# Attention head mixing feeding two feed-forward layers: one spread per head and chunk, and a new order of steps

## The chip, the cores and the metric

One core of a Trainium2 chip runs the whole program as one launch. The metric is the device time of one execution in microseconds (us). Engines are called PE or TensorE (matrix products), DVE or VectorE, ACT or ScalarE, POOL or GpSimd, and SP, whose queue issues most of the DMA transfers here.

## What is computed

```python
# q, k, v: (2, 12, 448, 64); w_pre, w_post: (12, 12)
scores = scale * np.matmul(q, k.transpose(0, 1, 3, 2))
scores = np.einsum('bhij,hg->bgij', scores, w_pre)
scores = scores - np.max(scores, axis=-1, keepdims=True)
attn = np.exp(scores)
attn = attn / (np.sum(attn, axis=-1, keepdims=True) + 1e-09)
attn = np.einsum('bhij,hg->bgij', attn, w_post)
attn_out = np.matmul(attn, v)             # then (896 tokens, 768)
# layer 1: h = x @ w_in (2048 wide), g = h * clip(h + 3, 0, 6) / 6, x = g @ w_out
# layer 2: h = x @ w_in, g = P(h) / (Q(h) + 1e-6) with a cubic P and a quadratic Q, out = g @ w_out
```

The 12 heads are mixed with each other before and after the softmax, for every pair of a query and a key.

## The kernel before, in words

The 448 queries of each batch are cut into chunks of 120, 120, 120 and 88 rows (the last padded to 90), eight chunks in all, called 0 to 7. A chunk is worked in groups of 10 queries: 12 groups, or 9 in chunks 3 and 7. A group has 120 rows on the partitions, 10 queries times 12 heads, so that a 120 x 120 block matrix mixes the heads in a matrix product.

Scores come out of TensorE head by head (queries on the partitions), and a group needs all heads of its queries side by side. `scores` (L233) computes a pair of heads, ScalarE and VectorE copy one head each into a staging tile `stg` (L249, L250), and `spread` (L227) sends that tile's rows by DMA to the rows of all groups. Before the change this takes two transfers for each head and chunk, one for each half of the groups:

```python
for f, (_, ng) in enumerate(spans[C]):
    to = halves[C][f].rearrange("(i h) g s -> h i g s", h=H)[h]
    nc.sync.dma_start(out=to[:, :ng], in_=st[f * HR : f * HR + ng * GR])
```

There are four `stg` buffers and three `half` tiles of six groups each. All spreads go through SP's queue, which issues in the order of the program; an issue waits until its staging tile is written.

The attention part is written out by hand as steps, one per group, in a manual schedule (from L513). Step m splits group m+2 into two float32r parts on GpSimd (`gsplit`, L255: `sh`, then `sl`), mixes group m in three products (`premix`, L270: tile `M`), takes its row maximum on VectorE (L279) and its exponential with the sum on ScalarE (L281), normalizes group m-2 on VectorE (`norm`, L286: `wr`), and mixes it again on TensorE (`postmix`, L297: tile `A`, copied to `at` by ScalarE). Into these steps tables put other work. `SST` (L510) tells at which steps of a chunk the six score pairs of the next chunk are computed (their copies and spreads follow one step later), `AVST` (L511) the six products of attention and values of the chunk before (`av_unit`, L317: tile `X`, a pair of heads each), and `QST` (L509) the split of the next chunk's queries. `k_prep` splits keys into `kst` tiles: batch 0 into XH, batch 1 into a tile of its own. Values are loaded as three tiles of four heads for a whole batch (`load_v`, L121).

The result of attention, x, must stand in XH and XL (two float32r parts) for the feed-forward layers. For chunks 0 and 1 it is first kept whole in `x1` (240 tokens, `XRAW`), since XH still holds keys, and split by `x_split` (L453, run in chunk 5); chunks 2 to 7 are split as they leave PSUM (L345, L346). In chunk 7 the first weights are loaded and split as well (`split_pieces`: two or three operations per piece on ScalarE, VectorE and GpSimd), and the first products of layer 1 begin. From there to the end the feed-forward layers run, which the change does not touch.

Of the kernel before, what the change touches and what calls it, by code (L numbers as in the profile page):

```python
# [30 lines left out]
def plan():  # L31

    chunks, halves = [], []
    for b in range(B):
        for c in range(NCH):
            n = min(CH, S - c * CH)
            G = (n + GR - 1) // GR
            chunks.append((b, c * CH, n, G))  # L40
# [6 lines left out]
def fused_kernel(  # L47
# [177 lines left out]
    halves = {}  # L225

    def spread(C, h, st):  # L227

        for f, (_, ng) in enumerate(spans[C]):
            to = halves[C][f].rearrange("(i h) g s -> h i g s", h=H)[h]  # L230
            nc.sync.dma_start(out=to[:, :ng], in_=st[f * HR : f * HR + ng * GR])  # L231

    def scores(C, hp, tags=("sc", "sc")):  # L233
# [613 lines left out]
```

## Time and profile before

| | us |
|---|---|
| median of 3 runs | 798.34 (797.26 to 799.27) |
| profiled execution | 793.91 |
| its span | 792.1 |
| first mixing product of group 0 starts | 33.85 |
| attention part ends (last values multiplied) | about 307 |
| TensorE busy in the span | 724.5 (91%) |
| VectorE, ScalarE, GpSimd busy | 567.2, 402.4, 258.0 |

Busy time of TensorE is modelled and an average over parts with different limits. The attention part is read step by step: a view of the waits or of the chain tells which engine's or queue's work ended last before a product could start.

### The profile page before, as it was taken

What the parts mean: (1) busy time and instruction counts of PE and PEld (TensorE: products, weight loads), DVE (VectorE), ACT (ScalarE), POOL (GpSimd) and SP (SyncE); (2) the same over time, 40 slices, a digit from 0 to 9 for tenths busy, and PEclk for the clock granted to TensorE, in tenths of its full rate; (3) what the DMA queues carried; (4) which work ended last, traced back from release to release, by engine and by line L of the source; (5) the groups of instructions that cost most, each with busy time, mean ns of one, the idle gap of its engine ahead of it and who ended that gap; (6) DMA issues with size and microseconds to landing.
All of it is one profiled execution on the core that took longest, in us unless ns stands there. A gap on an engine that the chain in (4) does not pass through costs nothing.

```text
span 792.1 us, 12221 instructions
## 1 busy us (share of the span) xinstructions
PE 724.5 (91%) x4457; PEld 621.5 (78%) x4457; DVE 567.2 (72%) x1036; ACT 402.4 (51%) x765; POOL 258.0 (33%) x255
## 2 busy tenths in 40 slices
PE   4397998889789889999999999999999998999986
PEld 2276776567577678888888888888999887999975
DVE  3366555366765576986674555568999999999996
ACT  3264555455555544444432111126676666689872
POOL 1275575465637581644442444420000000000000
PEclk9598999999999999999999999999999999999999
DMA  6631422324441512533332333323534343411002
GB/s 215 174 102 52 122 57 72 89 80 118 110 121 30 150 56 71 162 116 117 120 102 79 110 113 111 107 96 120 156 92 153 119 152 108 156 64 61 1 1 80
DMA packets 58747, 81.51 MB, mean 103 GB/s; under 512 B 5340, under 2 KB 54048, under 8 KB 58688
## 3 DMA queue, kind: packets, MB, share of 16 engines
q1 hardware_dynamic: 56768, 79.15, 32.7%
q10 hardware_dynamic: 1856, 1.58, 0.7%
q8 instruction: 35, 0.57, 0.3%
q14 instruction: 24, 0.20, 0.1%
q0 software_dynamic: 64, 0.01, 0.1%
HBM read 58.62 MB, written 2.75 MB: 77 GB/s over the span
## 4 chain that ended last, share of the span: by engine, by line
PE 58%; DVE 21%; DMA 10%; SPq 4%; issue 3%; ACT 3%; POOL 2%; POOLq 0%; ACTq 0%; DVEq 0%
PE h L355 8%; PE h L357 8%; PE h L356 8%; DMA half<-stg 6%; PE A L308 6%; PE y L355 5%; PE y L356 5%; PE y L357 5%; SPq L231 4%; PE X L328 3%; PE sc L246 3%; PE M L275 2%; DMA wraw<-in_moe_w_in_dram 2%; PE M L277 2%; DVE u L684 2%
## 5 line engine op out<-in xcount | busy, mean ns | idle before, releaser
L355 PE MATMUL h<-xh,wh 128*128 128x512 f32 (+1 forms) x384 | 141.6, 369 | 2.1 <-ACT wh L417 1.1
L357 PE MATMUL h<-xh,wl 128*128 128x512 f32 (+1 forms) x384 | 140.8, 368 | 2.1 <-DVE wl L418 2.1
L356 PE MATMUL h<-xl,wh 128*128 128x512 f32 (+1 forms) x384 | 140.7, 366 | 0.0
L281 ACT ACTIVATE e<-M,st 120x448 f32<-120x448 f32 x90 | 57.2, 635 | 105.5 <-DVE st L279 87.1
L308 PEld LDWEIGHTS A<-wr,e 120*112 120x112 f32 x720 | 87.6, 182 | 29.1 <-ACT at L312 8.0
L279 DVE TENSOR_REDUCE st<-M 120x1 f32<-120x448 f32 x90 | 56.0, 623 | 74.5 <-PE M L277 74.1
L308 PE MATMUL A<-wr,e 120*112 120x120 f32 x720 | 93.7, 275 | 14.8 <-DVE wr L292 12.8
L399 ACT ACTIVATE wf<-wraw 128x768 f32<-128x768 f32 (+1 forms) x50 | 43.7, 875 | 123.9 <-POOL wl L415 103.2
L265 POOL TENSOR_TENSOR sl<-half,sh 120x448 fp32r<-120x448 f32 x89 | 103.4, 1161 | 7.4
L263 POOL TENSOR_SCALAR sh<-half 120x448 fp32r<-120x448 f32 x89 | 54.8, 615 | 122.1 <-DMA half<-stg 69.9
L357 PEld LDWEIGHTS h<-xh,wl 128*128 128x128 f32 x384 | 72.1, 188 | 11.8 <-DVE wl L418 3.3
L355 PEld LDWEIGHTS h<-xh,wh 128*128 128x128 f32 x384 | 72.1, 188 | 11.5 <-ACT wh L417 1.9
L401 DVE TENSOR_SCALAR wf<-wf 128x768 int32<-128x768 int32 (+1 forms) x50 | 27.3, 546 | 74.4 <-ACT wf L399 74.1
L356 PEld LDWEIGHTS h<-xl,wh 128*128 128x128 f32 x384 | 72.1, 188 | 8.2
L414 POOL TENSOR_SCALAR wh<-wf 128x768 fp32r<-128x768 f32 (+1 forms) x34 | 33.4, 983 | 129.7 <-PE y L356 55.9
L355 PE MATMUL y<-gh,wh 128*128 128x384 f32 x192 | 70.6, 368 | 0.0
L356 PE MATMUL y<-gl,wh 128*128 128x384 f32 x192 | 70.2, 366 | 0.0
L357 PE MATMUL y<-gh,wl 128*128 128x384 f32 x192 | 69.7, 363 | 0.0
L415 POOL TENSOR_TENSOR wl<-wf,wh 128x768 fp32r<-128x768 f32 (+1 forms) x34 | 65.6, 1931 | 2.8
L275 PE MATMUL M<-sh,wp_h 120*120 120x448 f32 x90 | 43.0, 478 | 22.1 <-DVE sh L263 11.9
L312 ACT ACTIVATE at<-A 112x480 f32<-112x480 f32 x90 | 51.8, 576 | 4.4 <-PE A L308 4.0
L407 DVE SCALAR_TENSOR_TENSOR wf<-wraw,icst,wf 128x768 int32<-128x768 int32 (+1 forms) x50 | 50.5, 1012 | 0.8
(115 smaller groups left out, 1527.2 us busy)
## 6 DMA issues: line engine op xcount, KB each, us to landing
wraw<-in_moe_w_in_dram SPq DMA_DIRECT2D x30, 768.0 KB
wraw<-in_moe_w_out_dram SPq DMA_DIRECT2D x28, 768.0 KB
half<-stg SPq DMA_DIRECT2D x168, 105.0 KB
wraw<-in_moe_w_out_dram SPq DMA_DIRECT2D x6, 512.0 KB
kraw<-in_k_dram SPq DMA_DIRECT2D x6, 448.0 KB
vraw<-in_v_dram SPq DMA_DIRECT2D x6, 448.0 KB
qraw<-in_q_dram SPq DMA_DIRECT2D x6, 360.0 KB
wraw<-in_moe_w_in_dram ACTq DMA_DIRECT2D x2, 768.0 KB
```

Source lines behind the costliest of these rows:

```text
L263: eng.tensor_scalar(out=sh[:r], in0=s[:r], scalar1=1.0, scalar2=0.0, op0=ALU.mult, op1=ALU.add)
L265: return eng.tensor_tensor(out=sl[:r], in0=s[:r], in1=sh[:r].bitcast(F32), op=ALU.subtract)
L275: nc.tensor.matmul(mt[:r, :S], lhsT=a[:r, :r], rhs=sh[:r], start=True, stop=False)
L279: nc.vector.tensor_reduce(out=st[:r, 0:1], in_=mt[:r, :S], op=ALU.max, axis=AX.X, negate=True)
L281: nc.scalar.activation(out=e[:r], in_=mt[:r, :S], func=AF.Exp, bias=st[:r, 0:1], accum_out=st[:r, 1:2])
L308: nc.tensor.matmul(av[:, jc], lhsT=e[:r, jc * JP : (jc + 1) * JP], rhs=wr[:r, :, :rr], start=True, stop=True)
L312: lambda: nc.scalar.activation(out=at[C][:, :, :, c0 : c0 + rr], in_=av, func=AF.Copy)
L355: nc.tensor.matmul(o, lhsT=wh, rhs=mh, start=first, stop=False)
L356: nc.tensor.matmul(o, lhsT=wh, rhs=ml, start=False, stop=False)
L357: nc.tensor.matmul(o, lhsT=wl, rhs=mh, start=False, stop=last)
L407: nc.vector.scalar_tensor_tensor(out=wi, in0=lw, scalar=icst[:, 1:2], in1=wi, op0=ALU.logical_shift_right, op1=ALU.bitwise_or)
L415: nc.gpsimd.tensor_tensor(out=lv, in0=w, in1=hv.bitcast(F32), op=ALU.subtract)
```

## The change

Names: `full` is the tile that takes the place of the two `half` tiles, `stage` one tile for all heads of chunk 0.

- A chunk's groups stand in one tile `full` (two buffers), and a head's rows of a whole chunk go there in one transfer. Only chunk 0 still has two parts of six groups; its first part is sent first for all heads, eight heads by SP and four by ScalarE's queue.
- Scores of chunk 0 are staged at once in `stage`, which lies in one of the two `at` buffers. Later chunks stage a pair of heads in one tile of the tag `raw`, five buffers that the key loads share.
- Keys of batch 1 are split into XL, and loaded and split two pairs of heads at a time at steps 8 to 11 of chunks 0 to 2. So x stays whole in `x1` for chunks 0 to 5 (688 tokens). ScalarE makes the high part of the first 568 in chunk 6; the rest and the low part of all 688 follow in chunk 7.
- Values are loaded by pairs of heads for every chunk, each load behind the product that frees its buffer.
- The tables: score pairs at steps 0, 1, 3, 4, 6, 7 (of 9: 0 to 5), the queries of the chunk after next split at steps 8 and 9 (of 9: 6 and 7), value products at 2, 5, 8, 9, 11, 11. In a step VectorE's part of the copies now stands ahead of `premix`.

```diff
-            halves.append([(0, HG), (n - rest * GR, rest)])
+            parts.append([(0, G)] if chunks else [(0, HG), (HG, G - HG)])
...
-    XRAW = 2 * CH
+    XRAW = S + 2 * CH
...
-        t = front.tile([128, 2, S], F32, tag="raw", bufs=3, name=f"kraw{b}_{m}")
+        t = front.tile([128, 2, S], F32, tag="raw", bufs=5, name=f"kraw{b}_{m}")
...
-    def load_v(b, m):
-        t = att.tile([JP, 4, JC * D], F32, tag="vraw", bufs=3, name=f"vraw{b}_{m}")
+    def load_v(C, hp):
+        if C < len(chunks):
+            t = att.tile([JP, 2, JC * D], F32, tag="vraw", bufs=3, name=f"vraw{C}_{hp}")
+            nc.sync.dma_start(out=t, in_=v[chunks[C][0], hp])
...
-        front.tile([128, 2, NP, S], F32R, name="kst1"),
+    ksts = [x.rearrange("p c t -> p (c t)").rearrange("p (x h s) -> p x h s", x=2, s=S) for x in (XH, XL)]
...
+    def spread(C, h, st, part=0, eng=nc.sync):
+        g0, ng = parts[C][part]
+        to = full[C].rearrange("(i h) g s -> h i g s", h=H)[h]
+        eng.dma_start(out=to[:, g0 : g0 + ng], in_=st[g0 * GR : (g0 + ng) * GR])
...
-            halves[C] = [
-                att.tile([GP, HG, S], F32, tag="half", bufs=3, name=f"half{C}_{f}") for f in range(len(spans[C]))
-            ]
+            full[C] = att.tile([GP, MG, S], F32, tag="full", bufs=2, name=f"full{C}")
...
-        st = [front.tile([CH, S], F32, tag="stg", bufs=4, name=f"stg{C}_{2 * hp + i}") for i in range(2)]
+        if far:
+            st = front.tile([CH, 2, S], F32, tag="raw", bufs=5, name=f"stg{C}_{hp}")
...
+        load_v(*((C, h // 2 + 3) if h // 2 + 3 < NP else (C + 1, h // 2 + 3 - NP)))
         if h % 4 == 3:
             av_evac(C, h, X)
...
+    stage = att.tile([CH, H, S], F32, tag="at", bufs=2, name="stage")
     k_prep(0, 0)
     flush()
-    q_prep(0)
+    q_prep(0, 0, 1)
...
+        scores(0, hp, (("M", "A"), ("sc", "sc"))[hp % 2], stage[:, 2 * hp : 2 * hp + 2])
         flush()
+        if hp < 4:
+            for h in (2 * hp, 2 * hp + 1):
+                spread(0, h, stage[:, h])
+    for h in range(8, H):
+        spread(0, h, stage[:, h], 0, nc.scalar)
+    for h in range(H):
+        spread(0, h, stage[:, h], 1)
...
+    def x_hi(c, a, b):
+        nc.scalar.activation(out=XH[:, c, a:b], in_=x1[:, c, a:b], func=AF.Copy)
...
-            lambda: nc.scalar.activation(out=o, in_=x1[:, c, :], func=AF.Copy),
+            lambda: x_hi(c, XEAR, XRAW),
             lambda: nc.vector.tensor_tensor(
-                out=XL[:, c, :XRAW], in0=x1[:, c, :], in1=o.bitcast(F32), op=ALU.subtract
+                out=XL[:, c, :XRAW], in0=x1[:, c, :], in1=XH[:, c, :XRAW].bitcast(F32), op=ALU.subtract
...
-    QST = {12: 1, 9: 0}
-    SST = {12: [3, 4, 5, 6, 7, 8], 9: [3, 3, 4, 4, 5, 5]}
-    AVST = {12: [2, 2, 5, 9, 10, 11], 9: [2, 3, 5, 6, 8, 8]}
+    SST = {12: [0, 1, 3, 4, 6, 7], 9: [0, 1, 2, 3, 4, 5]}
+    QST = {12: [8, 9], 9: [6, 7]}
+    AVST = {12: [2, 5, 8, 9, 11, 11], 9: [2, 3, 5, 6, 8, 8]}
...
             gsplit(m + 2)
-            premix(m)
             for p in todo:
                 p[1]()
+            premix(m)
...
-            if C == NCH + 1 and s < KD:
+            if nxt is None and s < KD:
                 x_split(s)
+            if nxt == len(chunks) - 1 and s < KD:
+                x_hi(s, 0, XEAR)
```

The order of the instructions, at three places. **ScalarE at the start** (`sc` is a score tile, `qraw` and `kraw` are loaded queries and keys). Before:

```order
L249 ACTIVATE stg_0_142<-sc_0_140 120x448
L212 ACTIVATE xh<-kraw_2_107 128x448
L249 ACTIVATE stg_2_160<-sc_2_158 120x448
L212 ACTIVATE xh<-kraw_2_107 128x448
L249 ACTIVATE stg_4_178<-sc_4_176 120x448
L249 ACTIVATE stg_6_196<-sc_6_194 120x448
L221 ACTIVATE qr<-qraw_109 128x720
```

With the change:

```order
L212 ACTIVATE xh<-kraw_1_105 128x448
L249 COPY stage<-sc_0_131 120x448
L212 ACTIVATE xh<-kraw_1_105 128x448
L249 COPY stage<-sc_2_147 120x448
L212 ACTIVATE xh<-kraw_2_107 128x448 x2
L249 COPY stage<-sc_4_161 120x448
L249 COPY stage<-sc_6_175 120x448
L249 COPY stage<-sc_8_189 120x448
L231 DMA full_130<-stage 10x6x448
L249 COPY stage<-sc_10_201 120x448
L231 DMA full_130<-stage 10x6x448 x3
L221 ACTIVATE qr<-qraw_109 128x720
```

Four of chunk 0's first spreads now stand in ScalarE's own stream, behind its last copies; the other 20 stand in SP's.

**SP's queue in a later chunk** (the scores of chunk 2, computed during chunk 1). Before:

```order
L113 DMA qraw_746<-in_q_dram 128x6x90
L231 DMA half_0_734<-stg_0_738 10x6x448
L231 DMA half_1_735<-stg_0_738 10x6x448
L231 DMA half_0_734<-stg_1_739 10x6x448
L231 DMA half_1_735<-stg_1_739 10x6x448
```

With the change:

```order
L117 DMA qraw_585<-in_q_dram 128x6x90
L231 DMA full_611<-stg_0_614 10x12x448 x2
L231 DMA full_611<-stg_1_649 10x12x448 x2
L128 DMA vraw_3_692<-in_v_dram 112x512
L231 DMA full_611<-stg_2_718 10x12x448 x2
L231 DMA full_611<-stg_3_753 10x12x448 x2
L128 DMA vraw_4_794<-in_v_dram 112x512
```

A pair of heads takes two issues instead of four, and loads of values stand between them.

**VectorE in the last chunk**, around its steps 3 and 4. Before:

```order
L292 TENSOR_SCALAR wr_3202<-wq,st_3156 120x120
L279 TENSOR_REDUCE st_3212<-M_3208 120x1
L401 TENSOR_SCALAR wf<-wf 128x768
L403 SCALAR_TENSOR_TENSOR wf<-wraw,icst,wf 128x768
L289 TENSOR_SCALAR st_3178<-st_3178 120x1
L290 RECIPROCAL st_3178<-st_3178 120x1
L292 TENSOR_SCALAR wr_3235<-wq,st_3178 120x120
L279 TENSOR_REDUCE st_3245<-M_3241 120x1
```

With the change:

```order
L294 TENSOR_SCALAR wr_3125<-wq,st_3074 120x120
L478 TENSOR_TENSOR xl<-x_86,xh 128x688
L281 TENSOR_REDUCE st_3136<-M_3132 120x1
L406 TENSOR_SCALAR wf<-wf 128x768
L408 SCALAR_TENSOR_TENSOR wf<-wraw,icst,wf 128x768
L291 TENSOR_SCALAR st_3098<-st_3098 120x1
L292 RECIPROCAL st_3098<-st_3098 120x1
L294 TENSOR_SCALAR wr_3162<-wq,st_3098 120x120
L351 TENSOR_TENSOR xl<-X_1_3110,xh 128x2x120
L478 TENSOR_TENSOR xl<-x_86,xh 128x688
L281 TENSOR_REDUCE st_3174<-M_3170 120x1
```

A subtraction over 688 columns stands ahead of the reduce in six steps of this chunk.

## Rows read from the trace of the kernel before

**Rows 1.** The page: the engines' busy time (share of the span), and the clock that TensorE was granted in 40 equal slices (tenths of full speed).

```profile
PE 724.5 (91%) x4457; PEld 621.5 (78%) x4457; DVE 567.2 (72%) x1036; ACT 402.4 (51%) x765; POOL 258.0 (33%) x255
...
PEclk9598999999999999999999999999999999999999
```

**Rows 2.** The chain of waits around the change from chunk 1 to chunk 2: start, duration, what.

```profile
91.57 0.05 issue
91.62 0.75 SPq L231
...
97.41 2.55 DMA half<-stg
...
102.06 0.48 PE M L277
```

**Rows 3.** The tile view of `half`: the issues (duration in ns, least, median, most), and who waited for the tile and the spreads (us, times).

```profile
L231 SPq DMA_DIRECT2D half<-stg x192: 748/749/970, 11.5 to 269.5; - x192
...
  POOL sh L263: 69.9, 7
...
  DVE stg L250: 25.7, 18
  ACT stg L249: 23.9, 14
```

**Rows 4.** The DMA view: issues by kind, with the size of one.

```profile
half<-stg SPq DMA_DIRECT2D x168, 105.0 KB
...
half<-stg SPq DMA_DIRECT2D x24, 52.5 KB
```

**Rows 5.** SP's own timeline: start, time from the first to the last of a run of issues, line, what, how many.

```profile
43.77 20.25 SPq L231 DMA_DIRECT2D half<-stg  x24
```

**Rows 6.** Windows: stretch, its length, busy us of each engine (instructions), granted clock, busy share of the 16 DMA engines, GB/s. In this stretch SP issues spreads back to back.

```profile
28.00:32.00 4.00, 0.00 (x0) 0.00 (x0) 0.37 (x1) 0.00 (x0) 0.00 (x0) 0.50 0.45 134
```

**Rows 7.** The timeline of ScalarE at the start, then two rows of VectorE's: the split and the first reduce of group 0.

```profile
9.28 1.05 ACT L212 ACTIVATE xh<-kraw 128x448 fp32r<-128x448 f32 x2 [1.20 <-DMA kraw<-in_k_dram]
10.23 0.53 ACT L249 ACTIVATE stg<-sc 120x448 f32<-120x448 f32 x1
...
11.55 0.57 ACT L212 ACTIVATE xh<-kraw 128x448 fp32r<-128x448 f32 x1
17.65 0.54 ACT L249 ACTIVATE stg<-sc 120x448 f32<-120x448 f32 x1 [5.53 <-DMA half<-stg]
...
33.40 0.39 DVE L263 TENSOR_SCALAR sh<-half 120x448 fp32r<-120x448 f32 x1 [5.03 <-DMA half<-stg]
...
35.51 0.62 DVE L279 TENSOR_REDUCE st<-M 120x1 f32<-120x448 f32 x1 [0.82 <-PE M L277]
```

**Rows 8.** The pace of steps. TensorE's timeline: a step with a score pair (86.33 to 88.74), and one with a value pair (products `M` from 97.60, then `A`, then `X`). GpSimd's: the wait at the chunk change. VectorE's reduces: the first two of chunk 2, the first of chunk 6 and its tenth, and the first of chunk 7.

```profile
86.33 0.47 PE L275 MATMUL M<-sh,wp_h 120*120 120x448 f32 x1
...
88.74 0.46 PE L275 MATMUL M<-sh,wp_h 120*120 120x448 f32 x1
...
97.60 0.46 PE L275 MATMUL M<-sh,wp_h 120*120 120x448 f32 x1
...
99.22 1.04 PE L328 MATMUL X<-at,vraw 112*64 112x120 f32 x16
...
100.22 0.57 POOL L263 TENSOR_SCALAR sh<-half 120x448 fp32r<-120x448 f32 x1 [6.42 <-DMA half<-stg]
...
102.57 0.62 DVE L279 TENSOR_REDUCE st<-M 120x1 f32<-120x448 f32 x1 [2.87 <-PE M L277]
...
104.32 0.63 DVE L279 TENSOR_REDUCE st<-M 120x1 f32<-120x448 f32 x1
...
239.91 0.62 DVE L279 TENSOR_REDUCE st<-M 120x1 f32<-120x448 f32 x1 [3.90 <-PE M L277]
...
263.65 0.62 DVE L279 TENSOR_REDUCE st<-M 120x1 f32<-120x448 f32 x1 [0.58 <-PE M L277]
...
273.83 0.62 DVE L279 TENSOR_REDUCE st<-M 120x1 f32<-120x448 f32 x1 [3.25 <-PE M L277]
```

**Rows 9.** Windows of chunk 6 and of chunk 7 (columns as in rows 6: TensorE, weight loads, VectorE, ScalarE, GpSimd), then two lines of the source views (duration in ns, least, median, most) of subtractions on VectorE, and a row of VectorE's timeline in step 3 of chunk 7.

```profile
240.00:260.00 20.00, 19.40 (x161) 15.85 (x161) 13.60 (x37) 11.68 (x28) 13.92 (x17) 0.94 0.15 42
...
273.00:284.00 11.00, 9.20 (x79) 7.44 (x80) 7.83 (x20) 5.84 (x14) 10.25 (x13) 1.00 0.33 111
284.00:296.00 12.00, 10.14 (x87) 8.67 (x87) 9.21 (x22) 5.89 (x14) 9.09 (x9) 1.00 0.25 73
...
L457 DVE TENSOR_TENSOR xl<-x,xh x6: 886/1006/1372, 206.1 to 221.6; 128x240 fp32r<-128x240 f32 x6
...
L222 DVE TENSOR_TENSOR ql<-qraw,qr x8: 907/1116/1873, 8.1 to 245.1; 128x720 fp32r<-128x720 f32 x6, 128x540 fp32r<-128x540 f32 x2
...
281.32 1.78 DVE L403 SCALAR_TENSOR_TENSOR wf<-wraw,icst,wf 128x768 int32<-128x768 int32 x1
```

**Rows 10.** The issue of value loads (ns), two rows of the chain of waits (the six value products of the last chunk, and a load of weights), and a window of the feed-forward part.

```profile
L123 SPq DMA_DIRECT2D vraw<-in_v_dram x6: 352/418/1121, 32.5 to 200.6; - x6
...
303.65 3.79 PE X L328 x96
...
629.66 4.63 DMA wraw<-in_moe_w_in_dram
...
500.00:540.00 40.00, 40.00 (x200) 35.88 (x199) 22.75 (x31) 9.43 (x13) 10.00 (x7) 1.00 0.36 112
```

More of the change, by code (lines that the diff above doesn't have):

```diff
@@ L26 @@
 HG = 6
-HR = HG * GR
+MG = CH // GR
 NP = H // 2
 def plan():
-    chunks, halves = [], []
+    chunks, parts = [], []
     for b in range(B):
@@ L39, in plan, with row_of @@
             G = (n + GR - 1) // GR
+            parts.append([(0, G)] if chunks else [(0, HG), (HG, G - HG)])
             chunks.append((b, c * CH, n, G))
-            rest = G - HG
-            halves.append([(0, HG), (n - rest * GR, rest)])
-    return chunks, halves
+    return chunks, parts
+def row_of(chunk, g):
+    return min(g * GR, chunk[2] - GR)
 @with_exitstack
@@ L69, in fused_kernel @@
     GLAG = 1
-    chunks, spans = plan()
+    chunks, parts = plan()
     groups = [(C, g) for C, c in enumerate(chunks) for g in range(c[3])]
@@ L223, in q_prep, with scores @@
         )
[L225 to L233, printed above, removed]
+    full = {}
+    def spread(C, h, st, part=0, eng=nc.sync):
+        g0, ng = parts[C][part]
+        to = full[C].rearrange("(i h) g s -> h i g s", h=H)[h]
+        eng.dma_start(out=to[:, g0 : g0 + ng], in_=st[g0 * GR : (g0 + ng) * GR])
+    def scores(C, hp, tags=("sc", "sc"), st=None):
         n = chunks[C][3] * GR
@@ L246, in scores, with take @@
                 nc.tensor.matmul(sc[i][:n, :S], lhsT=w[o, hp, :n], rhs=x[o], start=(j == 0), stop=(j == 2))
-        post(
-            2,
-            lambda: (nc.scalar.activation(out=st[0][:n], in_=sc[0][:n, :S], func=AF.Copy), spread(C, 2 * hp, st[0])),
-            lambda: (nc.vector.tensor_copy(out=st[1][:n], in_=sc[1][:n, :S]), spread(C, 2 * hp + 1, st[1])),
-        )
+        def take(i, copy):
+            copy(out=st[:n, i], in_=sc[i][:n, :S])
+            if far:
+                spread(C, 2 * hp + i, st[:, i])
+        post(2, lambda: take(0, nc.scalar.copy), lambda: take(1, nc.vector.tensor_copy))
     ssp = {}
@@ L299, in postmix @@
         r, rr = GP, GR
-        c0 = spans[C][g // HG][0] + g % HG * GR
+        c0 = row_of(chunks[C], g)
         if g == 0:
@@ L341, in av_evac @@
         if t0 < XRAW:
-            xposts.append([lambda: None, lambda: nc.vector.tensor_copy(out=x1[:, cs, ts_], in_=src)])
+            take = [lambda: None, lambda: None]
+            take[h != 7] = lambda: (nc.vector.tensor_copy if h != 7 else nc.scalar.copy)(out=x1[:, cs, ts_], in_=src)
+            xposts.append(take)
         else:
@@ L524, in fused_kernel @@
         if nxt is not None:
-            if C > 0:
-                add([lambda: q_prep(nxt)], [QST[G]])
             add([lambda h=h: scores(nxt, h) for h in range(NP)], SST[G])
-        if C == 0:
-            add([lambda h=h: k_prep(1, h) for h in range(NP)], [0, 1, 2, 9, 10, 11])
+        if C + 2 < len(chunks):
+            add([lambda: q_prep(C + 2, 0, NP // 2), lambda: q_prep(C + 2, NP // 2, NP)], QST[G])
+        if C < 3:
+            add([lambda: load_k(1, C), lambda: k_prep(1, 2 * C), lambda: k_prep(1, 2 * C + 1)], [8, 10, 11])
         if C > 0:
@@ L539, in fused_kernel @@
         for s in range(G):
-            if s == 4 and C + 2 < len(chunks):
+            if s == 0 and C + 2 < len(chunks):
                 load_q(C + 2)
@@ L567, in fused_kernel @@
                 u()
-            if C == NCH and s == max(AVST[G]):
-                for i in range(3):
-                    load_v(1, i)
             if nxt is None and s == 0:
@@ L804, in _laid_out @@
     import numpy as _np
[L806 removed]
+    chunks, parts = plan()
     qt = _np.zeros((len(chunks), 2, D, NP, CH), q.dtype)
[L809 to L812 removed]
+    for C, (c, ps) in enumerate(zip(chunks, parts)):
+        for g0, ng in ps:
+            rows = [[c[1] + row_of(c, g0 + g) + i for g in range(ng)] for i in range(GR)]
+            rows = q[c[0], :, _np.array(rows).ravel()].reshape(ng * GR, NP, 2, D)
+            qt[C, ..., g0 * GR : (g0 + ng) * GR] = rows.transpose(2, 3, 1, 0)
     kt = k.reshape(B, NP, 2, S, D).transpose(0, 2, 4, 1, 3)
[L816 removed]
+    vt = v.reshape(B, NP, 2, JC, JP, D).transpose(0, 1, 4, 2, 3, 5)
     return {
```

35 lines of the change are left out of this document (13 added, 22 removed).

## The prediction

> **What bounds the kernel now.** I read the page first: TensorE is busy 91% of the span, and the clock line says where it isn't: the granted clock is 0.5 (the 1.2 GHz level) in the second slice, dips in the fourth, and is full later [rows 1]. So look at the attention part, from 0 to about 303 us. The chain of waits there, around one chunk change, reads: a reduce, then issue after issue on SP's queue, 0.75 us each, then a transfer of score rows, then GpSimd's split, and only then TensorE [rows 2]. The tile view of `half` sums it: 192 spreads; GpSimd waited 69.9 us for them in 7 places, the two engines that copy scores out 25.7 and 23.9 us for staging tiles still being sent [rows 3]. An issue takes 748 ns at least and 749 in the middle of all 192, though 168 move 60 rows of one head and 24 move 30 [rows 3, 4]: it costs by the piece, not by rows. SP's own timeline shows the queue saturated: 24 issues in 20.25 us from 43.77 [rows 5], against chunks of 34 us in which scores come only at steps 3 to 8. While it issues back to back the DMA engines are 0.45 busy [rows 6]. **SP's issues bound the attention part, not TensorE.**
>
> **The change, part by part.** The sum is made against the profiled execution, 793.91 us (span 792.10); the runs' median is 798.34, 0.6% above. I carry the saving over to the median.
>
> *First chunk.* Now group 0's split starts at 33.40, after 24 spreads through four staging buffers; ScalarE's third copy waited 5.53 us for one [rows 7]. After: 12 spreads carry groups 0 to 5, 8 issued by SP and 4 by ScalarE, and `stage` never blocks a copy. ScalarE is last: its first copy stays at about 10.2 (it follows the key load that lands at 9.28), then six copies at 0.53, three key splits at 0.57 and four issues at the 0.75 of SP's: 10.2 + 3.2 + 1.7 + 3.0 = 18.1, plus 2.6 from issue to landing [rows 2, 7]: 20.7, or **-12.7**. SP's eight end by 11.5 + 8 x 0.8 = 17.9 [rows 3]. Groups 6 to 11 follow on SP until about 28 and land by 31; group 6's split is due at step 4, 8 us after the first: covered. Bounds: if ScalarE's four cost as if on SP, 11.5 + 12 x 0.8 + 2.6 = 23.7 (-9.7); if ScalarE issues in half the time, -14.2.
>
> The DMA rule that the two queues end on the same 16 engines, so that a second issuer saves only sequencer time (the Trainium skill, DMA: Bandwidth & Descriptors, "Issuing engines are not separate DMA queues"), calls that time usually small; by it the ScalarE issues would bring nothing and this term would be -9.7. The trace disagrees: issuing is what fills the time, with the engines 0.45 busy [rows 6].
>
> *One spread per head and chunk.* 12 issues for 24. A 120-row issue isn't in the trace; the nearest rows (60 and 30 at the same price) give 0.75 [rows 3, 4]; the upper bound is twice that. The transfer's engine time doubles: 0.45 busy over 0.8 us becomes at most 0.8 x 0.9 = 0.72 us on 16 engines [rows 6]. So 12 take 9.6 us of SP per chunk, at the upper bound 18.6, where 24 took 20. SP also gets 6 value loads (0.42 each, [rows 10]) for each chunk, queued in the order of the attention-value products they wait for; behind them stand only spreads of later steps. 12 x 0.8 + 6 x 0.45 (with the gap between) + 0.9 for a query and a key load = 13 us in 30: SP is no longer full.
>
> On engine use, the Trainium skill (same page, "Why a DMA increments its semaphore by 16 and not by 1") lets a transfer use only as many engines as divide both outer sizes, here 10 for 120 rows onto 10 partitions. By it a spread takes 1.15 us and twelve 13.8, still under a chunk; the sum is unchanged, the upper bound comes nearer.
>
> *Step order.* Two whole `full` tiles let spreads begin at step 0, three steps (7 us) earlier, and the last pair is copied out at step 8: landed about 6.2 us into that step (copy 1.3, two issues 1.6, landing 2.6 + 0.7). GpSimd's split of the next group 0 is due 6 us into it and needed 5.2 us later: **the 6.4 us wait on GpSimd at a chunk change and its 2.9 us on VectorE go** [rows 2, 8]. The q split leaves the chunk's start for steps 8 and 9; the score copy stands before the reduce on VectorE, which waits for TensorE there anyway: nothing.
>
> What is late next is TensorE itself. Its undisturbed steps: with a score pair 86.33 to 88.74 = 2.41; with one value pair 1.62 + 1.0 = 2.6; with one of each 2.41 + 1.0 = 3.4, and with two value pairs taken as the same; with none 1.75, taken as 1.8 [rows 8]. A 12-step chunk after: 6 x 2.41 + 4 x 2.6 + 1.8 + 3.4 = 30.1; chunk 0 (no value products) 25.3; the 9-step chunk 3 x 2.41 + 3 x 3.4 + 2.6 + 1.8 + 3.4 = 25.2. Seven chunks: 25.3 + 5 x 30.1 + 25.2 = 201, against 273.83 - 35.51 = 238.3 now [rows 7, 8]. Such sums are a little short: nine steps from 239.91 took 23.7 where they give 22.4 [rows 8]. The first of them still refills after a stall, so I take half, 0.7 per nine steps: 6.3, in which chunk 0's first steps at the 1.2 GHz level (as now [rows 6]) must fit too. **-31**. Bounds: -37 without it; -20 if a third of the stalls stay.
>
> *Keys in XL, x kept raw.* Chunks 2 to 5 lose a subtraction each on VectorE and most of ScalarE's copies; chunk 6 gets six copies of 568 columns on ScalarE (some 0.7 each, as 448 take 0.57 [rows 7]; it is 11.7 of 20 us busy there [rows 9], so nothing). The last chunk gets six subtractions of 688 columns. The row of 240 columns took 0.89 to 1.37 with GpSimd running, the one of 720 0.91 to 1.87 [rows 9]: I take 1.4 each, 8.4 us. VectorE is busy 17.0 of 23 us there [rows 9], and its steps 3, 4 and 6 carry weight splits too, one of 1.78: they go above 4 us. **+5** of the 8.4, bounds 0 and +8.4.
>
> *The last values.* Three buffers hold one pair each, so pairs 3 to 5 of the last chunk load only when 0 to 2 are used. Six units take 3.79 us now [rows 10]. A load of 224 KB lands between the spread's 2.6 (105 KB) and the weights' 4.63 (768 KB) [rows 2, 10]: 2.9 by size. Unit 3 starts 0.63 + 0.1 + 0.42 + 2.9 = 4.0 in, not 1.9; less overlap of the later ones: **+1.7**, bounds 0 and +3. Behind it TensorE is full until 540 us [rows 10], so what the attention part gains or loses arrives at the end whole.
>
> Sum: -12.7 - 31 + 5 + 1.7 = **-37**: 757 by the profile, **761** on the median. Ends: -14.2 - 37 + 0 + 0 gives 747; -9.7 - 20 + 8.4 + 3 gives 780.
>
> **The rivals.**
> *A, issue grows with rows* (1.5 us). For it: a spread of 120 rows has twice the descriptors. Against: 30 and 60 rows cost the same. SP needs 18.6 + 3.6 of 30 us; the earlier start covers most, the 9-step chunk does not. About 1 us at six changes and 4 more in chunk 3: 771.
> *B, the floor is higher than TensorE's steps*: the small waits of copies, norms and splits behind each other cost 0.2 us in each of 81 steps. For it: the nine steps that ran over their sum by 1.3 us [rows 8]. 761 + 10 (0.2 x 81, less the 6.3 allowed): 771, with the last chunk's full 8.4: 775.
> *C, the split of group 0 still waits for all 24 first spreads.* Then it starts at 11.5 + 20 x 0.8 + 2.6 = 30.1, -3.3 in place of -12.7: 770. Against: it reads rows that only the first 12 write.
> *D, slower: the one big spread.* If issue and transfer of 120 rows follow each other without overlap, at 1.5 + 1.4 = 2.9 us, twelve take 35; with copy, landing and split (6) a chunk lasts 41 in place of 34: +7 x 6.8 - 6 = +42, 840. Against: issues now stand 0.05 us apart while transfers run under them [rows 2]. It decides from 2.4 us a spread: 12 x 2.4 + 6 = 34.8, where the rest's 6 us are used up.
> *E, ScalarE's issues save nothing*: its four and SP's next ones hold each other up. The first split comes at 23.7: 764. Against: the engines have room [rows 6].
> That the change doesn't do what it says is C.
>
> **How the numbers follow.** A measurement of this kernel tells 0.3% (2.4 us) from no change. Forecast 0.58 (752 to 768); A 0.10, B 0.12, C 0.06, D 0.04, E 0.08, anything near no change 0.02. Range 748 to 777: the forecast's own, E, and A, B and C with most of their width; it leaves out D and the far ends. Faster 0.94, same 0.02, slower 0.04.
>
> **What would show it.** Right: first reduce near 22.8 (35.5 now); issues of the 120-row spread at 0.75 to 0.8; GpSimd's waits for `full` under 10 us in sum; reduces of neighbouring chunks about 30 us apart and 25 in the 9-step one; no clock below 0.9 after 40 us; the last chunk 5 us longer, with VectorE as the releaser; a gap of 1 to 2 us between the last value units. Wrong: a spread issue well above 0.8, a first split near 30, steps with scores at 2.6 or more without a DMA wait.

## The result, and the profile after

The changed kernel takes 774.3 us (median of 4 runs, 771.24 to 776.24), the kernel before 797.8 beside it (4 runs, 797.09 to 799.27): ratio 0.970, 95% interval 0.9664 to 0.9735. It is faster, and the time lies in the range, but 23.5 us were saved where the forecast said 37. The profiled execution after took 776.24 (span 774.5), the longest of its four; the one of before (793.91) is shorter than all its four. So the two profiles differ by 17.6 only.

Where the time went, stage by stage. The marks are VectorE's row maxima (the first of each chunk) and the first 512-column product of layer 1; the last column runs to the span's end.

| us | to the first maximum | chunks 0 to 2 | chunks 3 to 6 | chunk 7, first to last maximum | to the first 512-column product | to the end |
|---|---|---|---|---|---|---|
| before | 35.5 | 99.8 | 138.5 | 22.2 | 13.0 | 483.0 |
| after | 23.4 | 98.8 | 118.9 | 29.7 | 17.6 | 486.1 |

The start saves 12.1 and chunks 3 to 6 save 19.6. Chunks 0 to 2 save 1.0 only, and 7.5, 4.6 and 3.1 are lost behind them.

The page after, as [rows 1]: TensorE is busy 94% now, and the clock dips in new places: most in the 14th slice (252 to 271 us), where chunk 7 runs, and again in the 34th, in layer 2.

```profile
PE 725.1 (94%) x4457; PEld 630.3 (81%) x4457; DVE 599.2 (77%) x1037; ACT 401.7 (52%) x772; POOL 256.1 (33%) x255
...
PEclk8799999999999799999999999999999998999998
```

What went as forecast: the tile view of `full` after (as [rows 3]; issues in ns, then waits in us and times), and SP's timeline (as [rows 5]), and VectorE's split and first maximum (as [rows 7]):

```profile
L231 SPq DMA_DIRECT2D full<-stg x84: 755/756/1267, 30.2 to 231.2; - x84
L231 SPq DMA_DIRECT2D full<-stage x20: 748/748/967, 9.7 to 27.8; - x20
L231 ACTq DMA_DIRECT2D full<-stage x4: 778/780/1550, 13.3 to 16.6; - x4
...
  DMA full<-stg: 5.7, 3
```

```profile
9.67 18.88 SPq L231 DMA_DIRECT2D full<-stage  x20
...
30.16 14.09 SPq L231 DMA_DIRECT2D full<-stg  x12
```

```profile
21.24 0.39 DVE L265 TENSOR_SCALAR sh<-full 120x448 fp32r<-120x448 f32 x1 [2.01 <-DMA full<-stage]
...
23.35 0.62 DVE L281 TENSOR_REDUCE st<-M 120x1 f32<-120x448 f32 x1 [0.82 <-PE M L279]
```

An issue of 120 rows takes 756 ns, as one of 60 or 30 did. GpSimd's 69.9 us for spreads [rows 3] held 30.1 at the start and 39.9 later; now it is 17.9 at the start and 5.7 later. Another 6.6 us, all ahead of a chunk's first group, are put down to loads of values and queries.

Then what did not. The end of chunk 0 after, steps 9 to 11: VectorE, ScalarE and TensorE (start, duration, what, in brackets the wait ahead of it).

```profile
48.75 0.53 DVE L222 TENSOR_TENSOR ql<-qraw,qr 128x360 fp32r<-128x360 f32 x1 [1.14 <-ACT qr L221]
49.20 0.62 DVE L281 TENSOR_REDUCE st<-M 120x1 f32<-120x448 f32 x1
...
51.59 1.56 DVE L213 TENSOR_TENSOR xl<-kraw,xl 128x448 fp32r<-128x448 f32 x1 [0.60 <-ACT xl L212]
53.08 0.61 DVE L281 TENSOR_REDUCE st<-M 120x1 f32<-120x448 f32 x1
```

```profile
49.91 0.64 ACT L283 ACTIVATE e<-M,st 120x448 f32<-120x448 f32 x1 [1.20 <-DVE st L291]
50.44 0.19 ACT L283 ACTIVATION_READ_ACCUMULATOR e<-M,st 120x1 f32 x1
50.53 0.57 ACT L314 ACTIVATE at<-A 112x480 f32<-112x480 f32 x1
50.99 0.57 ACT L212 ACTIVATE xl<-kraw 128x448 fp32r<-128x448 f32 x1
53.78 0.63 ACT L283 ACTIVATE e<-M,st 120x448 f32<-120x448 f32 x1 [2.23 <-DVE st L291]
```

```profile
51.14 1.04 PE L310 MATMUL A<-wr,e 120*112 120x120 f32 x8 [1.73 <-ACT at L314]
...
52.43 0.37 PE L279 MATMUL M<-sl,wp_h 120*120 120x448 f32 x1
55.02 1.05 PE L310 MATMUL A<-wr,e 120*112 120x120 f32 x8 [2.22 <-ACT at L314]
```

Read them as a ring. ScalarE's exponential (49.91) waits for VectorE; behind it on ScalarE stand the copy to `at` and the key split's high part (50.99). VectorE's low part (51.59) waits for that, and the next row maximum (53.08) stands behind the low part, although its product ended at 52.80. ScalarE's next exponential waits for the maximum (2.23), and TensorE for ScalarE (2.22). A step takes 3.9 us. VectorE's waits, first two lines of before, then after: the splits wait for ScalarE in more places, and the wait for the mixing product has shrunk, since the maximum comes late instead.

```profile
DVE st L279 <- PE M L277: 74.1, 60, 4.2
...
DVE ql L222 <- ACT qr L221: 4.3, 3, 3.4
```

```profile
DVE st L281 <- PE M L279: 14.4, 30, 0.9
DVE ql L222 <- ACT qr L221: 12.8, 15, 2.7
...
DVE xl L213 <- ACT xl L212: 5.2, 6, 1.6
DVE xl L478 <- ACT xh L473: 4.8, 4, 1.7
```

Chunk 7 after: a window (columns as in [rows 6, 9]), and step 3 on VectorE, with the subtraction of 688 columns ahead of the maximum, two weight pieces behind it, and then TensorE's wait.

```profile
241.00:271.00 30.00, 23.31 (x166) 19.16 (x165) 23.70 (x47) 12.92 (x34) 17.63 (x18) 0.83 0.40 115
```

```profile
250.44 0.87 DVE L478 TENSOR_TENSOR xl<-x,xh 128x688 fp32r<-128x688 f32 x1 [1.72 <-ACT xh L473]
251.23 0.62 DVE L281 TENSOR_REDUCE st<-M 120x1 f32<-120x448 f32 x1
251.76 0.79 DVE L406 TENSOR_SCALAR wf<-wf 128x768 int32<-128x768 int32 x1
252.59 1.76 DVE L408 SCALAR_TENSOR_TENSOR wf<-wraw,icst,wf 128x768 int32<-128x768 int32 x1
```

```profile
255.07 1.91 PE L310 MATMUL A<-wr,e 120*112 120x120 f32 x8 [3.39 <-DVE wr L294]
...
281.90 1.51 PE L330 MATMUL X<-at,vraw 112*64 112x88 f32 x32 [1.53 <-DMA vraw<-in_v_dram]
284.46 1.30 PE L330 MATMUL X<-at,vraw 112*64 112x88 f32 x16 [1.06 <-DMA vraw<-in_v_dram]
```

The eight products at 255.07 take 1.91 us, where eight took 1.05 at 55.02: ahead of them TensorE stood for 3.39 us, the granted clock is at its 1.2 GHz level, and the chunk's mean is 0.83. The last two rows are the forecast's gaps in the values.

### The profile page after: what moved, and what is told of

It reads as the page before. It is cut to its first block, busy times and chain, and to the rows that moved or that the text cites. A ratio compares the mean times of both kernels' runs of the same rounds, so it can differ in the third digit from the quotient of the medians.

```text
span 774.5 us, 12237 instructions
## 1 busy us (share of the span) xinstructions
PE 725.1 (94%) x4457; PEld 630.3 (81%) x4457; DVE 599.2 (77%) x1037; ACT 401.7 (52%) x772; POOL 256.1 (33%) x255
## 4 chain that ended last, share of the span: by engine, by line
PE 66%; DVE 21%; ACT 6%; DMA 4%; issue 2%; SPq 0%; DVEq 0%; ACTq 0%
PE h L360 8%; PE h L362 8%; PE h L361 8%; PE A L310 7%; PE y L360 5%; PE sc L246 5%; PE y L361 5%; PE y L362 5%; PE X L330 4%; PE M L277 3%; DVE st L281 2%; PE M L279 2%; ACT e L283 2%; PE M L278 2%; DVE u L706 2%
## 5 line engine op out<-in xcount | busy, mean ns | idle before, releaser
L360 PE MATMUL h<-xh,wh 128*128 128x512 f32 (+1 forms) x384 | 143.5, 374 | 2.1 <-DVE u L704 1.0
L362 PE MATMUL h<-xh,wl 128*128 128x512 f32 (+1 forms) x384 | 142.4, 372 | 2.1 <-DVE wl L423 2.1
L310 PEld LDWEIGHTS A<-wr,e 120*112 120x112 f32 x720 | 88.6, 182 | 33.4 <-ACT at L314 14.2
L310 PE MATMUL A<-wr,e 120*112 120x120 f32 x720 | 92.9, 274 | 22.1 <-DVE wr L294 14.3
L267 POOL TENSOR_TENSOR sl<-full,sh 120x448 fp32r<-120x448 f32 x89 | 103.8, 1166 | 7.4
L265 POOL TENSOR_SCALAR sh<-full 120x448 fp32r<-120x448 f32 x89 | 52.6, 591 | 95.9 <-PE M L278 64.3
L281 DVE TENSOR_REDUCE st<-M 120x1 f32<-120x448 f32 x90 | 55.9, 621 | 18.5 <-PE M L279 14.4
L294 DVE TENSOR_SCALAR wr<-wq,st 120x120 f32<-120x120 f32 x90 | 64.5, 717 | 3.2
## 6 DMA issues: line engine op xcount, KB each, us to landing
wraw<-in_moe_w_in_dram SPq DMA_DIRECT2D x30, 768.0 KB
wraw<-in_moe_w_out_dram SPq DMA_DIRECT2D x28, 768.0 KB
```

The costliest lines, as they stand in the source:

```text
L265: eng.tensor_scalar(out=sh[:r], in0=s[:r], scalar1=1.0, scalar2=0.0, op0=ALU.mult, op1=ALU.add)
L267: return eng.tensor_tensor(out=sl[:r], in0=s[:r], in1=sh[:r].bitcast(F32), op=ALU.subtract)
L281: nc.vector.tensor_reduce(out=st[:r, 0:1], in_=mt[:r, :S], op=ALU.max, axis=AX.X, negate=True)
L294: nc.vector.tensor_scalar(out=wr[:r], in0=wq[:r], scalar1=st[:r, 3:4], scalar2=None, op0=ALU.mult)
L310: nc.tensor.matmul(av[:, jc], lhsT=e[:r, jc * JP : (jc + 1) * JP], rhs=wr[:r, :, :rr], start=True, stop=True)
L360: nc.tensor.matmul(o, lhsT=wh, rhs=mh, start=first, stop=False)
```

## The experiments

Theory 1 is the ring. Theory 2: VectorE's `wr` (L294), 365 ns on average before and 717 after, stretches the steps. Theory 3: spreads land late. All ratios are to the kernel before, run beside each on the same chip; e1 to e3 and c0 shared one chip, e4 to e7 another, e8 to e10 a third, and e11 ran on a fourth. Stages are from one profile of each.

| kernel | median us (range) | ratio, 95% interval | chunks 0 to 2 | 3 to 6 | chunk 7 | to 512 columns |
|---|---|---|---|---|---|---|
| c0, as changed | 773.6 (769.9 to 775.8) | 0.9704, 0.966 to 0.975 | 97.2 | 118.9 | 29.7 | 16.4 |
| e1 | 765.4 (764.2 to 767.3) | 0.9608, 0.957 to 0.964 | 91.3 | 116.9 | 28.4 | 16.8 |
| e2 | 767.5 (764.8 to 769.6) | 0.9638, 0.959 to 0.969 | 91.6 | 116.9 | 28.3 | 18.0 |
| e3 = e2 + 4 value buffers | 762.4 (762.2 to 766.2) | 0.9579, 0.954 to 0.962 | 92.0 | 117.7 | 28.4 | 14.2 |
| e4 = e3 + early x split | 763.0 (762.6 to 763.3) | 0.9597, 0.958 to 0.961 | 90.7 | 119.6 | 27.6 | 14.7 |
| e5 = e3, all first spreads on SP | 762.5 (761.2 to 765.8) | 0.9596, 0.957 to 0.962 | 95.4 | 117.1 | 28.8 | 14.4 |
| e6 = e3, two spreads per head | 773.4 (770.3 to 774.5) | 0.9719, 0.969 to 0.975 | 97.4 | 117.9 | 29.7 | 14.2 |
| e7 = e3, old tables | 770.4 (768.0 to 771.0) | 0.9683, 0.966 to 0.970 | 96.7 | 120.0 | 28.5 | 14.5 |
| e8 = e3 without low part of x | 756.7 (755.0 to 757.3) | 0.9501, 0.945 to 0.955 | 90.9 | 116.9 | 22.9 | 14.4 |
| e9 = e3, x split apart | 762.7 (760.4 to 764.2) | 0.9577, 0.953 to 0.963 | 89.6 | 117.0 | 27.3 | 15.1 |
| e10 = e9 + 5 value buffers | 760.1 (758.7 to 763.1) | 0.9560, 0.950 to 0.962 | 90.4 | 117.2 | 27.5 | 14.2 |
| e11 = e10 + early x split | 762.0 (758.7 to 763.3) | 0.9588, 0.955 to 0.963 | 90.1 | 119.0 | 24.1 | 14.2 |

**c0, e1, e2: the ring.**

> The changed kernel once more, as the measure for the three beside it. All theories: 771 to 776 us, ratio to before 0.967 to 0.973.

```diff
# e1
-            for p in todo:
-                p[1]()
             premix(m)
+            for p in todo:
+                p[1]()
```

> Only the order inside a step is put back: all of VectorE's copies and subtractions stand behind the mixing product's row maximum again, as before the change; tables, spreads and buffers stay as changed. Theory 1 (a serial ring: a subtraction of the query, key or x split, which needs ScalarE's high part of the same step, holds up the row maximum, and ScalarE's next exponential behind it): chunks 0 to 2 take 87 to 90 us from first reduce to first reduce of chunk 3 in place of 98.9, the last chunk 3 to 5 us less; in all 10 to 14 us less than the changed kernel, 760 to 764, a little of it lost again because score copies leave later. Theory 2 (VectorE's normalization beside GpSimd's split, 717 ns in place of 365, is what stretches the steps): the row of the normalization stays near 700 ns and so do the chunks; within 3 us of the changed kernel, 771 to 776. Theory 3 (spreads land late in chunks 0 to 2): later copies make it worse, 775 to 785.

```diff
# e2: the subtractions carry a mark, p[2]
+            late = [p for p in todo if p[2:]]
             for p in todo:
-                p[1]()
+                if not p[2:]:
+                    p[1]()
             premix(m)
+            for p in late:
+                p[1]()
```

> Copies out of PSUM (scores, x of chunks 0 to 5) stay ahead of the row maximum as changed, but the subtractions of the query, key and x splits go behind it. Theory 1: as with everything behind it or up to 3 us better, since score copies and with them the spreads leave as early as in the changed kernel: 758 to 763; waits of the query and key subtractions on ScalarE no longer show a row maximum behind them, TensorE's gaps of 1.5 to 2.2 us in steps 8 to 11 of chunks 0 to 2 gone. Theory 2: within 3 us of the changed kernel. Theory 3: within 2 us of the changed kernel.

e1 takes 8.2 us off c0, e2 6.1, and chunks 0 to 2 fall by 5.9 and 5.6 (7.5 and 7.2 against the first profile of the changed kernel). That is theory 1, smaller than expected: chunks 0 to 2 were to take 87 to 90 us, and both totals lie 1.4 to 4.5 us above what was written down for them. The same place in e2 on VectorE; then from its waits, and `wr` from the groups (busy us, mean ns | idle before):

```profile
47.13 0.62 DVE L287 TENSOR_REDUCE st<-M 120x1 f32<-120x448 f32 x1
47.66 0.52 DVE L227 TENSOR_TENSOR ql<-qraw,qr 128x360 fp32r<-128x360 f32 x1
...
49.05 0.62 DVE L287 TENSOR_REDUCE st<-M 120x1 f32<-120x448 f32 x1 [0.29 <-PE M L285]
```

```profile
DVE ql L227 <- ACT qr L226: 3.5, 4, 2.8
```

```profile
L300 DVE TENSOR_SCALAR wr<-wq,st 120x120 f32<-120x120 f32 x90 | 60.5, 672 | 3.1
```

The step from 47.13 to 49.05 takes 1.9 us where the changed kernel needed 3.9 for the next one (49.20 to 53.08), and the query split's wait falls from 12.8 to 3.5. `wr` is about as slow as in the changed kernel (672 ns for 717; 424 in e1), and the gain is there in both: theory 2 falls. Theory 3 falls too, since e1 sends the spreads later and lost nothing. Whether copies stand ahead of the maximum (e2) or behind it (e1) makes no difference that the intervals show.

**e3: the last values.**

```diff
-            t = att.tile([JP, 2, JC * D], F32, tag="vraw", bufs=3, name=f"vraw{C}_{hp}")
+            t = att.tile([JP, 2, JC * D], F32, tag="vraw", bufs=4, name=f"vraw{C}_{hp}")
# each load four pairs ahead, four at the start
```

> The same with four value buffers in place of three, and loads four pairs ahead. If the two gaps of 1.5 and 1.1 us in the last values are the loads that wait for a free buffer, one of them goes or both shrink below 0.5: 1.5 to 3 us less than with three buffers, and if the fall of the clock behind them (0.52 for two products after) goes as well, up to 1 us more. If the loads are late for another reason (SP's queue), within 0.7 us.

The medians differ by 5.1 us. In the profiles the stretch behind the last maximum falls from 18.0 to 14.2: TensorE's wait for values shrinks from 1.68 to 0.93 us, and the granted clock over the stretch is 0.83 in e2 and 1.00 in e3, so most of the 3.8 is the clock of that one execution. e1, also with three buffers, has a wait of 1.62, a clock of 0.90 and a stretch of 16.8. The rest of the 5.1 has no place in these profiles: e3's is the longest of its four runs, and its span, 764.4, is no shorter than e2's 763.8.

**e6, e7: issue count or earlier start.**

```diff
# e6
-            parts.append([(0, G)] if chunks else [(0, HG), (HG, G - HG)])
+            parts.append([(0, HG), (HG, G - HG)])
...
-                spread(C, 2 * hp + i, st[:, i])
+                for part in (0, 1):
+                    spread(C, 2 * hp + i, st[:, i], part)
# e7
-    SST = {12: [0, 1, 3, 4, 6, 7], 9: [0, 1, 2, 3, 4, 5]}
-    QST = {12: [8, 9], 9: [6, 7]}
-    AVST = {12: [2, 5, 8, 9, 11, 11], 9: [2, 3, 5, 6, 8, 8]}
+    SST = {12: [3, 4, 5, 6, 7, 8], 9: [3, 3, 4, 4, 5, 5]}
+    QST = {12: [9, 10], 9: [6, 7]}
+    AVST = {12: [2, 2, 5, 9, 10, 11], 9: [2, 3, 5, 6, 8, 8]}
```

> The same as with four value buffers, but every head and chunk is sent in two transfers again (six groups and the rest), 24 a chunk, into the one tile and with the new tables. Theory issue count: the 24 issues take 18 us of SP again and bring back the stalls, chunks 33 to 34 us, 14 to 20 us more: 776 to 782. Theory earlier start: SP needs 24 x 0.8 + 3.5 = 22.7 of 30 us and starts three steps earlier, so chunks stay within 0.5 us of 30.5, total within 3 us, 762 to 765; only the 9-step chunk (22.7 of 26) may lose 2.

> The same as with four value buffers (one spread per head and chunk), but score pairs stand at steps 3 to 8 and value products at 2, 2, 5, 9, 10, 11 as before the change (the query split at steps 9 and 10). Theory issue count: twelve issues follow the copies without a queue, the last pair lands 6 to 6.5 us into step 9, 1 to 2 us late for the next chunk's first group: chunks 31 to 32, 5 to 9 us more, 767 to 771. Theory earlier start: stalls of 4 to 6 us at each change, on GpSimd for the spread tile, chunks 34 to 36, 24 to 35 us more: 786 to 797.

Two spreads cost 11.0 us, more than the theory of the earlier start allowed and less than that of the issue count; the old tables cost 8.0, as the issue count had it. In the profiles seven chunks take 215.3 and 216.7 us, against 209.7 in e3 and 238.3 before. So taking back either half loses only 5.6 or 7.0 of the 28.6 us that e3 gained there, and neither theory fits both runs. That fewer issues make a late start harmless, and that an early start hides many issues, would fit both, but it isn't shown: e6 and e7 both keep the two whole tiles and the five staging buffers, and no run takes back issues and tables together. In both the wait is back at the change from chunk 0 to 1, where e3's TensorE has one of 0.56 us; TensorE in e6 and e7:

```profile
52.48 0.46 PE L284 MATMUL M<-sh,wp_h 120*120 120x448 f32 x1 [3.54 <-POOL sh L272]
```

```profile
51.82 0.46 PE L283 MATMUL M<-sh,wp_h 120*120 120x448 f32 x1 [3.59 <-POOL sh L271]
```

The profile of e6 is the shortest of its four runs; its other 3 us have no place in it.

**e5: ScalarE's four issues.**

```diff
-        spread(0, h, stage[:, h], 0, nc.scalar)
+        spread(0, h, stage[:, h], 0)
```

> The same as with four value buffers, but the last four heads of chunk 0's first part are sent by SP's queue as all others, not by ScalarE's. If a second queue saves issue time (the forecast): first split at 23 to 24 in place of 21.3, so 1.7 to 3 us more: 764 to 765.5. If the transfers themselves are the limit (rival E of the prediction): first split within 0.7 us, total 762.4.

The medians are equal. From SP's first issue to the first split it is 12.2 us here (9.86 to 22.1) and 11.6 in e3 (10.57 to 22.2): ScalarE's issues save 0.6, not 3. In e3, and in the changed kernel as well, SP's sixth issue waits 2.3 us for a transfer into `full` while ScalarE's four are under way, and the first of those four takes 1.39 us (1.55 in the changed kernel) and not 0.78. e5 has no such wait. SP's own waits in e3 (us, times, longest):

```profile
SPq L237 <- DMA full<-stage: 2.3, 1, 2.3
```

That is what rival E said: ScalarE's four and SP's next ones hold each other up. SP begins at 9.7 to 10.6 and not at 11.5, as the prediction had it: twelve issues of 0.8 from 9.86 and 2.6 to landing make 22.1, as measured. In e5's profile GpSimd then waits 5.87 us for chunk 1's spreads; that run is the longest of its four, and whether the others had this wait isn't shown.

**e4, e8 to e11: the x split in chunk 7.**

```diff
# e4, e11: chunk 6, steps 8 to 11, rows 0 to 3
+            if nxt == len(chunks) - 1 and s >= 7 and s < 11:
+                xposts.append([lambda: None, lambda c=s - 7: x_lo(c, 0, XEAR), LATE])
# e8: 16 columns in place of 688
# e9, e10, e11: x_split(c) is queued at these steps (-1: the last step of chunk 6), and runs one later
+    XST = [-1, 0, 1, 3, 4, 6]
# e10, e11: vraw bufs=5, e bufs=3
```

> Copies first, subtractions behind the row maximum, four value buffers, and besides: the low part of x for the first 568 tokens is made in chunk 6, steps 8 to 11, for four of the six rows of x; the last chunk has 120 columns left for those. If VectorE's subtractions of 688 columns are what lengthens the last chunk (VectorE busy 23.9 of 28 us there): four of them fall from about 1.3 us to 0.3, last chunk 24 to 25.5 us in place of 28.4, 3 to 4 us less in all: 758.5 to 760 where the one without it has 762.4. Rival (chunk 6 pays it back, since its steps stand at TensorE's pace with little room): chunk 6 goes from 30.4 to 33, total 762. Rival (weight splits alone set the last chunk): last chunk 27.5 to 28.4, total 762.

> The version with copies first and four value buffers, in which the last chunk's subtractions of 688 columns are cut to 16 columns (the low part of x for chunks 0 to 5 is left out of the computation; all else, ScalarE's high parts too, stays). It prices the term that the prediction put at 5 us, bounds 0 and 8.4. If these subtractions set the last chunk: first to last reduce 22 to 23.5 us in place of 28.4, TensorE's gap of 2.7 us in the step with two weight pieces near 1.2 again, and one to two us more behind it, since the clock of the products after such a gap does not fall: 755 to 757. Rival (the last chunk is longer because weight splits, loads or the values changed): last chunk 27 to 28, total 761 to 762.

> Copies first, four value buffers, nothing left out: the six subtractions of 688 columns stand at steps 0, 1, 2, 4, 5 and 7 of the last chunk in place of 1 to 6, so that none shares a step with two pieces of the weight split on VectorE (steps 3 and 6). If it is the sum in those two steps that stops TensorE (2.7 and 2.0 us there with four buffers) and the clock falls behind it: last chunk 25 to 26 in place of 28.4, 758 to 760. If VectorE's whole work sets it (23.9 us busy of 28): last chunk 27.5 to 28.4, 761.5 to 762.5.

> The same with five value buffers in place of four, for which the exponentials have three buffers in place of four. If the gap of 0.9 to 1.3 us that is left in the last values is the load of a pair that waits for a buffer: it goes, 0.5 to 1.3 us less than with four. If the three buffers for the exponentials hold up ScalarE: steps longer by 0.1 or more each, 8 us more.

> The version with five value buffers and the subtractions apart, in which also the low part of the first 568 tokens is made in chunk 6, steps 8 to 11, for four of six rows. If VectorE's whole work sets the last chunk, taking four subtractions of about 1.3 us down to 0.3 there gives 24 to 25 us in place of 27.4, and chunk 6 pays 2 us back as it did before (32.3 in place of 30.4): 0.5 to 1.5 us less in all, 758.5 to 759.5. If chunk 6 pays all of it back: 760 or more.

e8 prices the term: without the subtractions chunk 7 takes 22.9 us, near the 22.2 before, at a full clock (its window: TensorE, weight loads, VectorE, ScalarE, GpSimd, then the clock), where e2's, shown below it, and e3's have 0.88:

```profile
231.00:254.00 23.00, 18.99 (x165) 15.75 (x164) 19.89 (x47) 12.86 (x34) 17.72 (x18) 1.00 0.51 145
```

```profile
232.00:261.00 29.00, 22.36 (x171) 18.47 (x169) 24.65 (x49) 12.98 (x35) 19.34 (x18) 0.88 0.43 121
```

VectorE has 4.8 us less to do than in e2, and the chunk is 5.5 shorter than in e3. No other edit got that back in the total. e9 took them out of the steps with two weight pieces and gained 1.1 in the chunk, nothing in the total: the waits moved to other steps (the longest now 2.46 us), as the theory of VectorE's whole work had it: VectorE is busy for 25.15 of 27.4 us, although the mean clock is 0.94. e4 paid 2.0 in chunk 6 (32.3 for 30.4) for 0.8 in chunk 7, since row 5 still met two weight pieces: TensorE waited, and the products behind it ran at the slow level (0.52 us where 0.34 is usual).

```profile
255.61 1.91 PE L316 MATMUL A<-wr,e 120*112 120x120 f32 x8 [2.92 <-DVE wr L300]
...
257.65 0.52 PE L368 MATMUL h<-xl,wh 128*128 128x384 f32 x1
```

e11, with both edits, has 24.1 us in chunk 7, but 2.0 more in chunk 6, and its total isn't apart from e10's. With five value buffers no wait over 0.5 us is left in the last values; the totals of e9 and e10 overlap. Of the kernels that leave nothing out, e10 has the lowest median (760.1, ratio 0.956). It is faster than both kernels, but its interval overlaps those of e3, e9 and e11.

## Why the prediction was right in sign and short in size

**The first chunk held.** Forecast -12.7 for the first split (20.7), measured 21.24; the first maximum came at 23.4 for 22.8. But the share given to ScalarE's issues was wrong: e5 puts it at 0.6 us and finds no difference in the total. By the Trainium skill (DMA: Bandwidth & Descriptors, "Issuing engines are not separate DMA queues") it should be small, and the trace agrees in the amount, though here it is SP's wait of 2.3 us that takes the saving back. The prediction argued against it, with a start of SP that was 1.8 us late; these two errors nearly made up for each other, which was luck. "ScalarE is last" was wrong as well: its fourth issue begins at 16.6, SP's eighth at 18.05. And the end of -14.2 was out of reach by the prediction's own figures, since SP's eight, ended at 17.9 and 2.6 us from landing, allow 20.5 (-12.9).

**The chunks: the step that failed** is the one costed at nothing: "the score copy stands before the reduce on VectorE, which waits for TensorE there anyway: nothing", with the query split sent to steps 8 and 9. The new order puts not only score copies ahead of the maximum but every subtraction of a split, and these wait for ScalarE in the same step. The cover that was named, VectorE's wait for TensorE, isn't there in steps 8 to 11 of chunks 0 to 2, where four splits follow each other. Forecast for seven chunks 207 (201 and 6.3 allowed), measured 217.7, and 208.5 with the order put back (e2). Chunks 3 to 6 fitted, 115.5 by the steps and 3.5 allowed make 119.0 for 118.9 measured, but partly by luck: e1 and e2 take 116.9, so 2.0 of it is the order again. For chunks 0 to 2 the sum was 88.3; 98.8 was measured, 91.6 in e2. Of the 3.3 that remain 2.4 lie in chunk 0, 28.6 for 26.2: its first two steps, at the 1.2 GHz level, take 2.81 each for 2.41, and its last takes 3.06 for 1.8, where GpSimd waits 3.11 us for a transfer before its first split for chunk 1. So a part of the wait that was to go at chunk changes is still there. No run takes these apart.

**Rival B** had the right total (771 to 775), not the right mechanism: it spread 0.2 us over each of 81 steps, but 7.0 of the 9.2 us between the changed kernel and e2 sat in twelve steps of three chunks, 4.0 of them in chunk 0.

**The last chunk** was forecast +5, bounds 0 and 8.4; it is +7.5, of which e2 takes 1.4 back (the ring) and e8 prices the subtractions at 5.5. VectorE as the releaser was right, and so, near enough, was the price of the subtractions; what the term left out is the ring. The granted clock is 1.00 in e8 and 0.83 after, but its share stays open: at 0.94, in e9, the chunk still takes 27.3.

**The last values**, forecast +1.7: the two gaps are 2.6 us, and with the slow clock behind them it is 4.6 in this profile. In c0, with gaps of 2.8 and the full clock, it is 3.4. Four buffers leave 1.2, and so do five.

**Behind them** the prediction carried the attention's gain to the end whole. This profile lost another 3.1 us there, for which see the last section; the stretch to the end lies between 484.2 and 487.8 in the twelve kernels above, which don't edit it, and the 483.0 before is below them all.

One sign named ahead failed outright: no clock below 0.9 after 40 us. It was 0.50 from 56 to 59 and from 125 to 127 us, where TensorE had just stood for 2.2 and 1.9; in e2 it is 1.00 from 30 to 240.

Against the 757 that the terms gave for the profile, 776.24 is 19.2 too long: 0.6 in the first chunk, 10.4 in the seven chunks (-20.6 for -31), 2.5 in the last chunk, 2.9 in the tail and 3.1 behind it make 19.5.

## What to carry to other kernels

When an order in a step changes, list for each instruction that moves ahead of a critical one which engine it waits for in the same step: an engine that "waits anyway" covers a copy, not an operation that depends on another engine's work of this step. Put the instruction that others wait for first, and side work with cross-engine inputs behind it. And where two edits may cure the same stall (fewer issues, an earlier start), take each back alone, and both together. Here one alone costs 11 or 8 us; the run without both is missing, so how they share the gain stays open.
